# Decode forward and backward on one core: operands kept in SBUF, mat-vecs and weight gradients moved to TensorE

## The chip, the core and the metric

The kernel runs on one core of a Trainium2 chip. The metric is device microseconds (us) of that core. Each kernel is run several times and the median is quoted. A run counts as fast when it lies within 1.5% of the fastest run of the same kernel. A single run of a kernel has the state "unknown" and is used here only for readings of its trace. In the text PE is TensorE, PEld its weight load, DVE VectorE, ACT ScalarE, POOL GpSimd and SP SyncE. "The clock" is the share of TensorE's full clock that was granted, as the trace records it: 0.50 or 1.00 in nearly every stretch below.

## The reference

One token passes through attention, MLP, the same attention and the same MLP again (called A1, B2, A3, B4 below). Then the gradients of everything are taken. All tensors are bf16.

```python
def _A_ref(x, k_cache, v_cache, wq, wo):          # D 1024, 32 heads of 128, 4 KV heads, cache of 32768
    W = 4096                                      # only the last 4096 positions of the cache are used
    q = (x @ wq).reshape(B, Sq, Hq, Dh).transpose(0, 2, 1, 3)
    k = jnp.repeat(k_cache[:, :, Sk - W:, :], rep, axis=1)
    v = jnp.repeat(v_cache[:, :, Sk - W:, :], rep, axis=1)
    p = softmax(einsum("bhqd,bhkd->bhqk", q, k) * Dh ** -0.5)
    return einsum("bhqk,bhkd->bhqd", p, v).transpose(...).reshape(B, Sq, Hq * Dh) @ wo
def _B_ref(x, w1, b1, w2):                        # F 3584
    h = x @ w1 + b1
    return (h * tanh(softplus(h))) @ w2
x = x + _A_ref(layernorm(x), ...); x = x + _B_ref(layernorm(x), ...)     # and both once more
# outputs: x, and the gradients of x, k_cache, v_cache, wq, wo, w1, b1, w2 for a given grad_out
```

Three facts shape the work. Every product with a weight is a mat-vec. Every weight gradient is a sum of two outer products, one for each use of the weight, so it has rank two. And 58.7 MB of the gradients of the two caches, those of the positions that were not used, are zeros that must be written.

## The kernel before

In the forward part the mat-vecs were already done on PE, 128 columns of weight at a time. In the backward part they were products and sums along the free axis, on DVE and ACT, because there the contraction runs along the other axis of the weight. Each weight was loaded anew at every use, and K and V were loaded three times each, twice as they are and once transposed by the DMA.

```python
    # forward, for example q: a chunk of weight, 32 matmuls of one column each
    for t in range(TD):
        chunk = wpool.tile([P, J], BF16, name="wq_chunk")
        nc.sync.dma_start(chunk[:], wq_v[:, t, :])
        for h in range(HQ):
            nc.tensor.matmul(q_ps[:, c:c + 1], lhsT=chunk[:, h * P:(h + 1) * P], rhs=n_bf[:, t:t + 1], ...)
    # ... (cut)
    # backward: a mat-vec is a product with a broadcast row, summed by DVE, or by ACT after DVE
    def mv_accum(in0, in1, acc, n, prodpool):
        path = MV_PATTERN[mv_state[0] % len(MV_PATTERN)]          # "BABBA"
        if path == "A":
            nc.vector.tensor_tensor_reduce(out=prod[:, 0:n], in0=in0, in1=in1, ..., accum_out=acc)
        else:
            nc.vector.tensor_tensor(out=prod[:, 0:n], in0=in0, in1=in1, op=ALU.mult)
            nc.scalar.activation(prod[:, 0:n], prod[:, 0:n], ACT.Copy, accum_out=acc)
    # ... (cut)
    # a weight gradient: one pass of ACT, one of DVE, one output DMA
    def dw_block(ot, bc_hi, sc_hi, bc_lo, sc_lo, out_ap):
        nc.scalar.activation(ot, bc_hi, ACT.Copy, scale=sc_hi)
        nc.vector.scalar_tensor_tensor(out=ot, in0=bc_lo, scalar=sc_lo, in1=ot, op0=ALU.mult, op1=ALU.add)
        eng.dma_start(out_ap, ot)
```

Of the kernel before, what the change touches and what calls it, by code (L numbers as in the profile page):

```python
# [12 lines left out]
AX = mybir.AxisListType  # L13

# [3 lines left out]


def prow(h: int) -> int:  # L20
    return 32 * (h // 8) + (h % 8)
# [3 lines left out]
def kernel(  # L25
# [23 lines left out]

    D = A_x.shape[2]  # L50
    assert D % P == 0
    TD = D // P
    G = A_k_cache.shape[1]
    Sk = A_k_cache.shape[2]
    assert A_k_cache.shape[3] == DH
    assert G == 4, "kernel assumes 4 kv heads (one quadrant per group)"
    W = min(4096, max(256, Sk // 4))
    assert W % P == 0
    SC = min(512, W)
    assert W % SC == 0  # L60
    TK = W // P
    J = A_wq.shape[1]
    assert J == HQ * DH
    F = B_w1.shape[1]
    assert F % 512 == 0
    TF = F // P
    ZR = Sk - W
    assert ZR % P == 0
    scale = float(DH) ** -0.5
    eps = 1e-5  # L70
    invD = 1.0 / D

    keep = ctx.enter_context(tc.tile_pool(name="keep", bufs=1))
    ps1 = ctx.enter_context(tc.tile_pool(name="ps1", bufs=4, space=bass.MemoryType.PSUM))

    ident_bf = keep.tile([P, P], BF16, name="ident_bf")
# [3 lines left out]
    ones_f = keep.tile([P, P], FP32, name="ones_f")  # L80
    nc.vector.memset(ones_f[:], 1.0)
    ones_bf = keep.tile([P, P], BF16, name="ones_bf")
    nc.vector.memset(ones_bf[:], 1.0)
    eps_t = keep.tile([P, 1], FP32, name="eps_t")
    nc.vector.memset(eps_t[:], eps)


    KVT = keep.tile([P, G, W], BF16, name="KVT")

    zero_jobs = []  # L90
    if ZR > 0:
        per_part_z = ZR // P * DH
        for out_t in (out_2, out_3):
            for g in range(G):
                zero_jobs.append((out_t, g))

    def write_zero_regions(src_tile, njobs, name):
        if ZR == 0 or not zero_jobs or njobs == 0:
            return
        ZC = 1024 if per_part_z % 1024 == 0 else min(D, per_part_z)  # L100
        assert per_part_z % ZC == 0 and src_tile.shape[1] >= ZC
        zt = keep.tile([P, ZC], BF16, name=f"zt_{name}")
        nc.vector.tensor_scalar(out=zt[:], in0=src_tile[:, 0:ZC], scalar1=0.0, scalar2=None, op0=ALU.mult)
        reps = per_part_z // ZC
        for _ in range(njobs):
            if not zero_jobs:
                break
            out_t, g = zero_jobs.pop(0)
            dst = out_t[0, g, 0:ZR, :].rearrange("(p r) d -> p (r d)", p=P)
            nc.gpsimd.dma_start(dst.rearrange("p (r c) -> p r c", c=ZC), zt[:, None, :].to_broadcast([P, reps, ZC]))  # L110

    def load_col_f32(ap_flat, name):
        tb = keep.tile([P, TD], BF16, name=name + "_bf")
        nc.sync.dma_start(tb[:], ap_flat.rearrange("(t p) -> p t", p=P))
        tf = keep.tile([P, TD], FP32, name=name)
        nc.vector.tensor_copy(tf[:], tb[:])
        return tf

    x0 = load_col_f32(A_x[0, 0, :], "x0")
    gcol = load_col_f32(grad_out[0, 0, :], "gcol")  # L120

    b1_bf = keep.tile([P, TF], BF16, name="b1_bf")
    nc.sync.dma_start(b1_bf[:], B_b1.rearrange("(t p) -> p t", p=P))
    b1_f = keep.tile([P, TF], FP32, name="b1_f")
    nc.vector.tensor_copy(b1_f[:], b1_bf[:])

    db1_acc = keep.tile([P, TF], FP32, name="db1_acc")
    nc.vector.memset(db1_acc[:], 0.0)
# [4 lines left out]
    w2_v = B_w2.rearrange("(t p) d -> p t d", p=P)  # L133

    def ln_fwd(x_col, name):
        with tc.tile_pool(name=f"ln_{name}", bufs=1) as lp, tc.tile_pool(
            name=f"lnps_{name}", bufs=1, space=bass.MemoryType.PSUM
        ) as lps:
            xx = lp.tile([P, 2 * TD], FP32, name="xx")
            nc.vector.tensor_copy(xx[:, 0:TD], x_col[:])  # L140
            nc.vector.tensor_mul(xx[:, TD:2 * TD], x_col[:], x_col[:])
            sps = lps.tile([P, 2 * TD], FP32, name="sps")
            nc.tensor.matmul(sps[:], lhsT=ones_f[:], rhs=xx[:], start=True, stop=True)
            s12 = lp.tile([P, 2], FP32, name="s12")
            nc.vector.reduce_sum(s12[:], sps[:].rearrange("p (a b) -> p a b", a=2), axis=AX.X)
            mean = lp.tile([P, 1], FP32, name="mean")
            nc.vector.tensor_scalar(out=mean[:], in0=s12[:, 0:1], scalar1=invD, scalar2=None, op0=ALU.mult)
            msq = lp.tile([P, 1], FP32, name="msq")
            nc.vector.tensor_mul(msq[:], mean[:], mean[:])
            var = lp.tile([P, 1], FP32, name="var")  # L150
            nc.vector.scalar_tensor_tensor(out=var[:], in0=s12[:, 1:2], scalar=invD, in1=msq[:], op0=ALU.mult, op1=ALU.subtract)  # L151
            rstd = keep.tile([P, 1], FP32, name=f"rstd_{name}")
            nc.scalar.activation(rstd[:], var[:], ACT.Sqrt, bias=eps_t[:, 0:1], scale=1.0)  # L153
            nc.vector.reciprocal(rstd[:], rstd[:])
            n32 = keep.tile([P, TD], FP32, name=f"n32_{name}")
            nc.vector.tensor_scalar(out=n32[:], in0=x_col[:], scalar1=mean[:, 0:1], scalar2=rstd[:, 0:1], op0=ALU.subtract, op1=ALU.mult)
            n_bf = keep.tile([P, TD], BF16, name=f"nbf_{name}")
            nc.vector.tensor_copy(n_bf[:], n32[:])
        return n32, n_bf, rstd

    def ln_bwd(dn_col, n32, rstd, name):
        with tc.tile_pool(name=f"lnb_{name}", bufs=1) as lp, tc.tile_pool(
            name=f"lnbps_{name}", bufs=1, space=bass.MemoryType.PSUM
        ) as lps:
            tt = lp.tile([P, 2 * TD], FP32, name="tt")
            nc.vector.tensor_copy(tt[:, 0:TD], dn_col[:])
            nc.vector.tensor_mul(tt[:, TD:2 * TD], dn_col[:], n32[:])  # L167
            sps = lps.tile([P, 2 * TD], FP32, name="sps")
            nc.tensor.matmul(sps[:], lhsT=ones_f[:], rhs=tt[:], start=True, stop=True)  # L169
            ab = lp.tile([P, 2], FP32, name="ab")  # L170
            nc.vector.reduce_sum(ab[:], sps[:].rearrange("p (a b) -> p a b", a=2), axis=AX.X)
            nc.vector.tensor_scalar(out=ab[:], in0=ab[:], scalar1=invD, scalar2=None, op0=ALU.mult)
            nb = lp.tile([P, TD], FP32, name="nb")
            nc.vector.tensor_scalar(out=nb[:], in0=n32[:], scalar1=ab[:, 1:2], scalar2=None, op0=ALU.mult)
            t2 = lp.tile([P, TD], FP32, name="t2")
            nc.vector.tensor_sub(t2[:], dn_col[:], nb[:])
            gx = lp.tile([P, TD], FP32, name="gx")
            nc.vector.tensor_scalar(out=gx[:], in0=t2[:], scalar1=ab[:, 0:1], scalar2=rstd[:, 0:1], op0=ALU.subtract, op1=ALU.mult)
            gx_keep = keep.tile([P, TD], FP32, name=f"gx_{name}")
            nc.vector.tensor_copy(gx_keep[:], gx[:])  # L180
        return gx_keep

    def col_to_row(col_bf, ncols, dst_row_ap, rng, name):
        with tc.tile_pool(name=f"c2r_{name}", bufs=1, space=bass.MemoryType.PSUM) as rps:
            rowps = rps.tile([P, ncols * P], BF16, name="rowps")
            for c in range(ncols):
                nc.tensor.transpose(rowps[rng:rng + 1, c * P:(c + 1) * P], col_bf[:, c:c + 1], ident_bf[:], tile_position=(0, rng))
            nc.vector.tensor_copy(dst_row_ap[rng:rng + 1, :], rowps[rng:rng + 1, :])

    def col_to_row_mapped(colpad_bf, dst_row_ap, rng, name):  # L190
        with tc.tile_pool(name=f"c2rm_{name}", bufs=1, space=bass.MemoryType.PSUM) as rps:
            rowps = rps.tile([P, HQ * P], BF16, name="rowps")
            for h in range(HQ):
                c = prow(h)
                nc.tensor.transpose(rowps[rng:rng + 1, h * P:(h + 1) * P], colpad_bf[:, c:c + 1], ident_bf[:], tile_position=(0, rng))
            nc.vector.tensor_copy(dst_row_ap[rng:rng + 1, :], rowps[rng:rng + 1, :])

    def row_to_bcast(src_row_ap, rng, length, dst_bc, name):
        CB = min(512, length)
        assert length % CB == 0  # L200
        with tc.tile_pool(name=f"bc_{name}", bufs=2, space=bass.MemoryType.PSUM) as bps:
# [21 lines left out]
    def attn_fwd(x_col, lname, stack_row_n, stack_row_o, load_kt=False):  # L223
# [5 lines left out]
        with tc.tile_pool(name=f"qf_{lname}", bufs=1) as qp, tc.tile_pool(  # L229
# [16 lines left out]
            for g in range(G):  # L246
                nc.tensor.transpose(rows_ps[32 * g:32 * g + 32, :], qs_col[:, 32 * g:32 * g + 32], ident_bf[:], tile_position=(0, 32 * g))
# [433 lines left out]
```

## Time and profile before

| | before |
|---|---|
| time, median (lowest to highest) | 989.47 us (988.42 to 991.69), 3 runs |
| forward, backward, gradients | 0 to 323, 323 to 820, 820 to 991 us |
| bytes moved | 250.16 MB |
| busiest engine | DVE, 45% of the span |

First, lines of the profile's page. The rows of digits cut the span into 40 slices; a digit is the busy share of that slice in tenths (for PEclk, the clock in tenths). GB/s is what the DMA moved in each slice. The lines that start with L are groups of instructions: busy us, mean ns of one, then the idle time just before them and what ended it.

```profile
PE 270.3 (27%) x3388; PEld 197.5 (20%) x3388; DVE 446.1 (45%) x666; ACT 363.9 (37%) x568; POOL 17.7 (2%) x24
...
PEclk9956555567555555555655555555556755555555
...
GB/s 307 239 49 210 309 229 326 330 212 156 299 268 298 173 418 421 179 393 418 201 88 337 167 417 415 147 216 310 408 333 85 189 235 70 228 232 190 195 179 223
DMA packets 114187, 250.16 MB, mean 252 GB/s; under 512 B 48097, under 2 KB 48097, under 8 KB 105953
...
L459 ACT ACTIVATE mv_prod<-mv_prod 128x1024 bf16<-128x1024 bf16 (+2 forms) x91 | 137.8, 1515 | 182.5 <-DVE mv_prod L458 179.6
...
L563 DVE SCALAR_TENSOR_TENSOR dwo_ot<-gbcA_A_4276,ocol_A_740,dwo_ot 128x1024 bf16<-128x1024 bf16 x32 | 40.5, 1281 | 12.4 <-ACT dwo_ot L562 12.2
```

No engine is busy for half of the span, and the DMA reaches 415 GB/s and more in only five of 40 slices. The backward mat-vecs are the group at L459 with its DVE partner; the weight gradients are groups like L563, in which DVE waits for ACT.

Second, windows of the trace of before. Each row is a stretch of time: its bounds, its length, then busy us and number of instructions of PE, PEld, DVE, ACT and POOL, then the clock, the DMA share and GB/s.

```profile
66.00:78.00 12.00, 12.00 (x55) 5.98 (x55) 3.07 (x14) 3.69 (x14) 0.00 (x0) 0.50 0.01 1
...
234.00:240.00 6.00, 3.12 (x54) 2.94 (x54) 0.00 (x0) 0.00 (x0) 0.00 (x0) 1.00 0.62 238
360.00:396.00 36.00, 3.78 (x28) 2.89 (x28) 14.99 (x25) 18.22 (x25) 0.00 (x0) 0.50 1.03 420
820.00:991.00 171.00, 68.51 (x510) 54.01 (x508) 131.37 (x161) 126.45 (x239) 4.28 (x8) 0.50 0.55 191
```

Between 66 and 78 us TensorE does transposes in turn with small matmuls, each transpose with a copy before its result can be used, and the clock is 0.50. Between 360 and 396 us the DMA is full, at 420 GB/s, with zero writes beside loads. The gradients take 171 us with DVE and ACT busy for three quarters of it and the DMA about half used.

### The profile page before, as it was taken

What the parts mean: (1) busy time and instruction counts of PE and PEld (TensorE: products, weight loads), DVE (VectorE), ACT (ScalarE), POOL (GpSimd) and SP (SyncE); (2) the same over time, 40 slices, a digit from 0 to 9 for tenths busy, and PEclk for the clock granted to TensorE, in tenths of its full rate; (3) what the DMA queues carried; (4) which work ended last, traced back from release to release, by engine and by line L of the source; (5) the groups of instructions that cost most, each with busy time, mean ns of one, the idle gap of its engine ahead of it and who ended that gap; (6) DMA issues with size and microseconds to landing.
All of it is one profiled execution on the core that took longest, in us unless ns stands there. A gap on an engine that the chain in (4) does not pass through costs nothing. (4 is left out here: it accounts for less than half of the span.)

```text
span 991.2 us, 8850 instructions
## 1 busy us (share of the span) xinstructions
PE 270.3 (27%) x3388; PEld 197.5 (20%) x3388; DVE 446.1 (45%) x666; ACT 363.9 (37%) x568; POOL 17.7 (2%) x24
## 2 busy tenths in 40 slices
PE   2436323436322001000390001000005702234553
PEld 2224222314222001000160001000002501223432
DVE  1040101040010344764517545487644196897777
ACT  0030010020010236643116433336531256867776
POOL 0000000000000100010000100001000000000000
PEclk9956555567555555555655555555556755555555
DMA  8915868894878999599428499958982465554545
GB/s 307 239 49 210 309 229 326 330 212 156 299 268 298 173 418 421 179 393 418 201 88 337 167 417 415 147 216 310 408 333 85 189 235 70 228 232 190 195 179 223
DMA packets 114187, 250.16 MB, mean 252 GB/s; under 512 B 48097, under 2 KB 48097, under 8 KB 105953
## 3 DMA queue, kind: packets, MB, share of 16 engines
q1 hardware_dynamic: 93056, 166.76, 51.1%
q0 software_dynamic: 15616, 67.11, 16.6%
q10 hardware_dynamic: 5472, 15.73, 4.1%
q8 instruction: 26, 0.43, 0.2%
q14 instruction: 17, 0.13, 0.0%
HBM read 142.62 MB, written 98.58 MB: 243 GB/s over the span
## 5 line engine op out<-in xcount | busy, mean ns | idle before, releaser
L459 ACT ACTIVATE mv_prod<-mv_prod 128x1024 bf16<-128x1024 bf16 (+2 forms) x91 | 137.8, 1515 | 182.5 <-DVE mv_prod L458 179.6
L607 PE MATMUL kv_ps<-qsrows_A_1663,ds_A_3438 8*128 8x128 bf16 x128 | 29.8, 283 | 66.7 <-ACT kv_otile L612 33.6
L563 DVE SCALAR_TENSOR_TENSOR dwo_ot<-gbcA_A_4276,ocol_A_740,dwo_ot 128x1024 bf16<-128x1024 bf16 x32 | 40.5, 1281 | 12.4 <-ACT dwo_ot L562 12.2
L563 DVE SCALAR_TENSOR_TENSOR dwq_ot<-dqbc_A_4716,n_A_114,dwq_ot 128x4096 bf16<-128x4096 bf16 x8 | 35.8, 4480 | 9.7 <-ACT dwq_ot L562 9.7
L562 ACT ACTIVATE dwo_ot<-gbcA_A_3445,ocol_A_2278 128x1024 bf16<-128x1024 bf16 x32 | 36.2, 1152 | 10.6 <-DMA out_dram<-dwo_ot 10.6
L563 DVE SCALAR_TENSOR_TENSOR dwo_ot<-gbc_B_4017,a_B_1360,dwo_ot 128x1024 bf16<-128x1024 bf16 x28 | 35.6, 1282 | 9.7 <-ACT dwo_ot L562 9.5
L169 PE MATMUL sps<-tt,ones_f 128*128 128x16 f32 x8 | 2.3, 370 | 136.0 <-DVE tt L167 136.0
L563 DVE SCALAR_TENSOR_TENSOR dw_ot<-dhbc_B_4149,n_B_1072,dw_ot 128x3584 bf16<-128x3584 bf16 x8 | 31.6, 3949 | 16.6 <-ACT dw_ot L562 16.6
L612 ACT CAST kv_otile<-kv_ps 128x128 bf16<-128x128 f32 x170 | 35.2, 269 | 10.3 <-PE kv_ps L608 4.0
L219 PE MATMUL bfc_ps<-ident_bf,dh_bf 128*128 128x128 bf16 x56 | 7.5, 303 | 113.6 <-DVE dh_bf L429 61.8
L490 PE MATMUL dorows_ps<-ident_bf,do_col 128*32 128x128 bf16 x8 | 0.6, 288 | 133.8 <-DVE do_col L486 133.8
L607 PE MATMUL kv_ps<-dorows_A_3439,pbf_4866 8*128 8x128 bf16 x128 | 29.4, 286 | 28.0 <-DVE kv_otile L610 15.4
L153 ACT ACT_TABLE_LOAD x4 | 5.1, 1283 | 86.0 <-DVE var L151 85.3
L562 ACT ACTIVATE dw_ot<-dhbc_B_3317,n_B_2614 128x3584 bf16<-128x3584 bf16 x8 | 26.2, 3276 | 26.8 <-DMA out_dram<-dw_ot 26.7
L562 ACT ACTIVATE dwo_ot<-gbc_B_3185,a_B_2902 128x1024 bf16<-128x1024 bf16 x28 | 32.1, 1156 | 7.5 <-DMA out_dram<-dwo_ot 7.3
L523 PE MATMUL dq_ps<-kn,dsT_all 128*32 128x128 bf16 x256 | 33.3, 284 | 3.5 <-DMA kn<-in_A_k_cache_dram 3.2
L562 ACT ACTIVATE dwq_ot<-dqbc_A_3884,n_A_1656 128x4096 bf16<-128x4096 bf16 x8 | 29.7, 3714 | 11.8 <-DMA out_dram<-dwq_ot 11.1
L608 PEld LDWEIGHTS <-ds_A_4269 8*128 8x128 bf16 x128 | 19.1, 149 | 74.3 <-issue 73.5
L294 PE MATMUL o_ps<-vn,pT_all 128*32 128x128 bf16 x256 | 31.9, 271 | 4.6 <-DMA vn<-in_A_v_cache_dram 4.6
L608 PE MATMUL kv_ps<-qsrows_A_121,ds_A_4269 8*128 8x128 bf16 x128 | 32.4, 308 | 0.0
L608 PE MATMUL kv_ps<-dorows_A_4270,pbf_4868 8*128 8x128 bf16 x128 | 31.5, 307 | 0.0
L169 PEld LDWEIGHTS sps<-tt,ones_f 128*128 128x128 f32 x8 | 2.0, 311 | 136.8 <-issue 75.6
(266 smaller groups left out, 762.7 us busy)
## 6 DMA issues: line engine op xcount, KB each, us to landing
wq_chunk<-in_A_wq_dram SPq DMA_DIRECT2D x32, 1024.0 KB, 7.0
wo_chunk<-in_A_wo_dram SPq DMA_DIRECT2D x32, 1024.0 KB, 8.5
w_chunk<-in_B_w_dram SPq DMA_DIRECT2D x32, 896.0 KB, 6.7
w_chunk<-in_B_w_dram SPq DMA_DIRECT2D x28, 1024.0 KB, 8.8
out_dram<-zt_B_3202 POOLq DMA_DIRECT2D x2, 7168.0 KB, 56.4
out_dram<-zt_A_3462 POOLq DMA_DIRECT2D x2, 7168.0 KB, 42.3
out_dram<-zt_B_4034 POOLq DMA_DIRECT2D x2, 7168.0 KB, 44.9
out_dram<-zt_A_4293 POOLq DMA_DIRECT2D x2, 7168.0 KB, 46.1
```

The lines of the kernel that those rows point to most:

```text
L153: nc.scalar.activation(rstd[:], var[:], ACT.Sqrt, bias=eps_t[:, 0:1], scale=1.0)
L169: nc.tensor.matmul(sps[:], lhsT=ones_f[:], rhs=tt[:], start=True, stop=True)
L219: nc.tensor.matmul(bp[:, i * P:(i + 1) * P], lhsT=col_bf[:, src:src + 1].to_broadcast([P, P]), rhs=ident_bf[:], start=True, stop=True, til ...
L294: nc.tensor.matmul(o_ps[32 * g:32 * g + 32, :], lhsT=pT_all[:, t, 32 * g:32 * g + 32], rhs=vn[:, t, :], start=(t == 0), stop=(t == TK - 1) ...
L459: nc.scalar.activation(prod[:, 0:n], prod[:, 0:n], ACT.Copy, accum_out=acc)
L490: nc.tensor.transpose(rows_ps[32 * g:32 * g + 32, :], do_col[:, 32 * g:32 * g + 32], ident_bf[:], tile_position=(0, 32 * g))
L523: nc.tensor.matmul(dq_ps[32 * g:32 * g + 32, :], lhsT=dsT_all[:, t, 32 * g:32 * g + 32], rhs=kn[:, t, :], start=(t == 0), stop=(t == TK - ...
L562: nc.scalar.activation(ot, bc_hi, ACT.Copy, scale=sc_hi)
L563: nc.vector.scalar_tensor_tensor(out=ot, in0=bc_lo, scalar=sc_lo, in1=ot, op0=ALU.mult, op1=ALU.add)
L607: nc.tensor.matmul(ps[:], lhsT=X3[32 * g:32 * g + 8, t:W:TK], rhs=Y3[32 * g:32 * g + 8, :], start=True, stop=False, tile_position=(32 * g, 0))
L608: nc.tensor.matmul(ps[:], lhsT=X1[32 * g:32 * g + 8, t:W:TK], rhs=Y1[32 * g:32 * g + 8, :], start=False, stop=True, tile_position=(32 * g, 0))
L612: nc.scalar.copy(otile[:, t, :], ps[:])
```

## The change

The intent is to load wq, K and V once and keep them in SBUF, to transpose weights in place on PE where the other layout is wanted, so that the backward mat-vecs are PE work too, and to make each weight gradient by a matmul whose contraction is over two rows. DVE and ACT then only copy results out of PSUM. The diff rewrites nearly the whole kernel; its core is this.

```diff
+    def xpose_unit(ap2d, nb):                     # transposes 8 blocks, copies them back over themselves
+        ps = pt.tile([P, 8, P], BF16, name="tps", tag="pt")
+        for b in range(nb):
+            nc.tensor.transpose(ps[:, b, :], ap2d[:, b * P:(b + 1) * P], ident_bf[:])
+        evac(ap2d, ps[:, 0:nb, :].rearrange("p b c -> p (b c)"), 0.08 * nb, 0.12 * nb)    # DVE or ACT
     # ... (cut) attention forward
+        if first:
+            load_wq()
+            load_kv(K_t, k_v, "K")
     # ... (cut) at the end of each attention forward
+        for c in range(HQ // 2):
+            w = strm.tile([P, 2, D], BF16, name="wo_c", tag="st")
+            nc.sync.dma_start(w[:], wo_v[:, 2 * c:2 * c + 2, :])
+            if c == NB - 1:
+                zeros(10)                         # ten of 56 zero writes of 1 MB, in pieces of 1 KB
     # ... (cut) a backward mat-vec: load, transpose, one-column matmuls
-                        mv_accum(chunk[:, tt, :], gbc[:], da[:, t:t + 1], D, prodpool)
+            for tt in range(2):
+                xpose_unit(w[:, tt, :], 8)
+            for tt in range(2):
+                t = 2 * c + tt
+                for dch in range(TD):
+                    mm(dacc[:, t:t + 1], w[:, tt, dch * P:(dch + 1) * P], g_bf[:, dch:dch + 1], dch == 0, dch == TD - 1)
     # ... (cut) gradients: the two vectors of each weight lie in two rows of ROWS
+    ROWS = keep.tile([P, 5120], BF16, name="ROWS")
-        nc.scalar.activation(ot, bc_hi, ACT.Copy, scale=sc_hi)
-        nc.vector.scalar_tensor_tensor(out=ot, in0=bc_lo, scalar=sc_lo, in1=ot, op0=ALU.mult, op1=ALU.add)
+                mm(ps[:], ROWS[base:base + 2, (r0 + rr) * P:(r0 + rr + 1) * P], ROWS[base:base + 2, L + i * 512:L + (i + 1) * 512],
+                   True, True, tile_position=(base, 0))
+                ev_out(st[:, rr, i * 512:(i + 1) * 512], ps[:])
     # ... (cut) order of the end
+    zeros(100)                                    # all that are left
+    to_row(sB4["a_bf"], TF, 96, 0, "a4")          # column -> row, by a small DMA into ROWS
     # ... (cut)
+    for t in range(0, TF, 2):
+        dw_tall(96, t, 4096, out_8.rearrange("(t p) d -> p t d", p=P), "w2")
     # ... (cut) then w1, wo, V, K and wq, each with its own to_row calls just ahead
```

## The prediction

> **What bounds the kernel now.** No single engine: the summary page shows DVE busy 45% of 991 us, ACT 37%, PE 27%. The stage windows show three regimes.
> - Forward, 0 to 323 us: mat-vec stages run at the DMA ceiling. A chunk of 32 column mat-vecs takes 1.02 us (31.5 ns each, at granted clock 0.5 and 1.0 alike) and then PE waits for the next chunk. Windows full of loads move 380 to 422 GB/s. Each attention adds about 50 us with little DMA (4096-column softmax, 64 transposes handed over one by one).
> - Backward, 323 to 820 us: mat-vecs are products on DVE and ACT (1.22 us, or 0.69 + 1.24 us, per 128x1024 block; 128x4096 costs 4.42 us). Zero writes beside loads fill windows at 415 to 420 GB/s and starve DVE; wq and w1 stages are DVE-bound; the attention middle (744 to 792 us) has little DMA.
> - Gradients, 820 to 991 us: each block needs an ACT pass (1.15 us per 128x1024) and a DVE pass (1.28 us), alternating with output DMA in the chain of waits. DMA is half used.
>
> **What the change does.**
> - Traffic falls from 250 MB (DMA view) to about 204 MB: wq, K, V once (17 MB), streamed wo, w1, w2 89 MB, zeros 59 MB, outputs 40 MB. At the 418 GB/s seen here: 488 us, the floor.
> - Backward mat-vecs go to TensorE: 1920 more at 31.5 ns = 60 us, but each block first needs a transpose: about 2050 in all. Eight back-to-back 128-column matmuls (the broadcasts) took 1.04 us at clock 0.5, so about 107 ns each at half clock: 220 us; 120 us if the clock is granted. Evacuating 128x1024 bf16 from PSUM, extrapolated from 225 ns (DVE) and 266 ns (ACT) for 128 columns, is 0.69 and 1.0 us; shared, 0.41 us per 8 transposes, below PE.
> - Attention middles shrink: 1024-column softmax rows, a fourth of the exp and reduction time.
> - Gradients: 312 evacuations of 512 columns (0.69 us DVE, 0.59 us ACT): 99 us shared. PE 160 us at half clock, 80 us at full.
>
> The Trainium skill, "TensorE: Matmul & The Clock Gate", Part 4, says that transposes do not bring the full clock. This trace agrees weakly: interleaved transposes (66 to 78 us) stayed at 0.50 with PE busy throughout, while plain dense matmuls (234 to 240 us) reached 1.0. I assume half clock in the backward streams.
>
> **Sum of estimates (us):** A1 forward 90 (36 MB with ten zero writes, DMA-bound), B2 36, A3 48, B4 36: 210. Backward MLPs 30 chunks x 2.3 = 69 + 6 each; A3 backward 37 (wo) + 58 (resident transposes) + 33; A1 backward 70: about 350, PE-bound, zeros hidden below. Gradients 100 to 150, partly overlapped. Total about 670; with full clock about 560. I take 640.
>
> **What would show it.** Forward windows at 400 GB/s or more with PE waiting for DMA; backward windows with PE near full, clock 0.5, DMA under half, transposes near 107 ns apart; gradients with DVE and ACT near full; total DMA near 204 MB; PE the largest share in the chain of waits.
>
> **What would make it wrong.** Full clock during transposes (then 560); transposes waiting for evacuation with only four PSUM buffers, or mat-vecs waiting in order behind copies (700 or more); rank-2 matmuls at half clock setting the last phase; 512 KB loads falling short of 400 GB/s.
>
> Predicted 640 us, 80% range 560 to 735. Faster by over 2%: 0.98; within 2%: 0.01; slower: 0.01.

## The result, and the profile after

| | before | after |
|---|---|---|
| time, median (lowest to highest) | 989.11 us (988.42 to 991.69), 4 runs | 653.39 us (652.58 to 653.72), 4 runs |
| forward | 323 us | 225 us |
| backward | 497 us | 230 us |
| gradients | 171 us | 197 us |
| bytes moved | 250.16 MB | 205.10 MB |

The ratio is 0.6595, with a 95% interval of 0.6579 to 0.661. The ratios here and below are those of fast runs over fast runs; they are not quite the ratios of the medians in the tables. The time of before differs a little from the first table because a fourth run was added with the result. The results are correct.

The total was predicted within 14 us. The stages were not: the backward part was predicted at about 350 us, and the gradients at 100 to 150. The last stage even became 26 us longer than the one it replaced.

The same lines of the page, for after:

```profile
PE 451.2 (69%) x7117; PEld 325.0 (50%) x7117; DVE 242.1 (37%) x470; ACT 203.4 (31%) x292; POOL 62.3 (10%) x109
...
PEclk9985555555555599989975999995555555555555
...
GB/s 307 425 415 383 388 286 390 388 386 383 388 387 392 252 281 333 296 283 382 382 390 153 289 288 298 304 384 382 384 390 195 289 185 309 218 195 139 153 224 292
DMA packets 118215, 205.10 MB, mean 315 GB/s; under 512 B 11514, under 2 KB 68992, under 8 KB 117120
...
L145 PE MATMUL ops<-ROWS 2*128 2x512 bf16 (+1 forms) x248 | 104.8, 606 | 29.8 <-DMA ROWS<-rt 26.3
...
L138 PE MATMUL tps<-ident_bf,w_c 128*128 128x128 bf16 x896 | 72.1, 225 | 0.0
L133 ACT COPY w_c<-tps 128x896 bf16<-128x896 bf16 (+1 forms) x48 | 45.8, 955 | 79.7 <-PE tps L138 74.6
L130 DVE COPY w_c<-tps 128x1024 bf16<-128x1024 bf16 (+1 forms) x72 | 47.0, 656 | 46.1 <-PE tps L138 35.2
```

PE is now the busiest engine. The row PEclk has the main surprise in it: digits of 7 to 9, with one 5 between, from the 15th to the 27th slice, and nothing but 5 after that. A slice is 16.3 us, so these are the backward stages (228 to 440 us). The clock was full where the prediction took half, and half where PE had the most to do. The group at L145 is the weight gradients: PE stood still before them for 29.8 us, and 26.3 us of that ended with a small copy into ROWS.

The windows of after, with the columns as above:

```profile
12.00:24.00 12.00, 4.97 (x140) 4.23 (x136) 0.00 (x0) 0.00 (x0) 0.00 (x0) 1.00 1.03 420
60.00:84.00 24.00, 0.00 (x0) 0.00 (x0) 0.00 (x0) 0.00 (x0) 0.00 (x0) 0.50 1.08 389
240.00:324.00 84.00, 76.60 (x1538) 69.65 (x1535) 50.13 (x85) 47.94 (x51) 0.00 (x0) 0.98 0.98 338
312.00:324.00 12.00, 12.00 (x219) 12.00 (x217) 10.69 (x18) 10.16 (x12) 0.00 (x0) 1.00 1.09 383
336.00:348.00 12.00, 9.45 (x336) 9.14 (x334) 0.69 (x1) 0.20 (x1) 0.00 (x0) 0.50 0.99 366
360.00:432.00 72.00, 60.73 (x1272) 51.58 (x1269) 34.24 (x61) 33.03 (x34) 0.00 (x0) 1.00 0.92 306
504.00:516.00 12.00, 12.00 (x33) 4.48 (x32) 9.26 (x16) 8.82 (x17) 3.82 (x7) 0.50 0.61 240
588.00:612.00 24.00, 24.00 (x127) 16.32 (x124) 10.20 (x17) 9.80 (x17) 5.25 (x8) 0.50 0.46 167
```

Read them in order. In the forward part the DMA is full and PE waits for it; between 60 and 84 us PE does nothing at all, because the next chunk's load stands behind ten zero writes. From 240 to 324 and from 360 to 432 us PE is busy for five sixths and more, at full clock. From 312 to 324 us it does only the transposes of resident operands: 219 instructions in 12 us are 55 ns each. From 336 to 348 us it does almost only matmuls of one column (for wq) or eight (for K), and the clock is back at 0.50. In the gradients, 504 to 516 and 588 to 612 us, PE is busy without a gap, and the clock is 0.50 all the same.

The timeline of PE in the trace of after, at the start of the backward part (start, us, engine and operation, number):

```profile
225.83 2.85 PE L138 MATMUL tps<-ident_bf,w_c 128*128 128x128 bf16 x25
228.47 0.40 PE L145 MATMUL acc<-gcolb,w_c 128*128 128x1 bf16 x8
...
230.14 0.77 PE L138 MATMUL tps<-ident_bf,w_c 128*128 128x128 bf16 x11
...
231.14 0.38 PE L138 MATMUL tps<-ident_bf,w_c 128*128 128x128 bf16 x4
```

One transpose alone takes 0.27 us at half clock and 0.22 us at full clock, from its start to its end; the next one starts sooner than that. The first 25 take 2.85 us, so they start about 107 ns apart. Later eleven take 0.77 us and four 0.38 us, so they start about 55 ns apart. In windows of 1 us the clock is 0.50 up to 229 us, 0.67 in the next and 1.00 from 230 us, about 4 us after the first transpose; the work until then was transposes with a few one-column mat-vecs between them. From 302 to 330 us PE does nothing but transposes, and the clock stays at 1.00 (the window 312 to 324 us above), so transposes alone keep it there.

The end of the chain of waits of after, in order of time (start, us, what):

```profile
615.97 2.36 DMA ROWS<-rt
...
618.58 27.37 PE ops L145 x64
```

The last weight's 64 matmuls take 27.37 us, so they follow each other every 0.43 us, behind a copy of its rows. Nothing else is in the chain there: it is PE alone that sets the pace.

### The profile page after: what moved, and what is told of

The parts are those of the page before. It is cut to its first block, busy times and chain, and to the rows that moved or that the text cites. A ratio compares the mean times of both kernels' runs of the same rounds, so it can differ in the third digit from the quotient of the medians.

```text
span 652.0 us, 16240 instructions
## 1 busy us (share of the span) xinstructions
PE 451.2 (69%) x7117; PEld 325.0 (50%) x7117; DVE 242.1 (37%) x470; ACT 203.4 (31%) x292; POOL 62.3 (10%) x109
## 2 busy tenths in 40 slices
DMA packets 118215, 205.10 MB, mean 315 GB/s; under 512 B 11514, under 2 KB 68992, under 8 KB 117120
## 5 line engine op out<-in xcount | busy, mean ns | idle before, releaser
L145 PE MATMUL ops<-ROWS 2*128 2x512 bf16 (+1 forms) x248 | 104.8, 606 | 29.8 <-DMA ROWS<-rt 26.3
L145 PEld LDWEIGHTS <-w_c 128*128 128x128 bf16 x1792 | 60.2, 101 | 67.3 <-DMA w_c<-in_B_w_dram 40.5
L145 PEld LDWEIGHTS <-ROWS 2*128 2x128 bf16 x248 | 33.6, 137 | 99.7 <-issue 88.9
L138 PE MATMUL tps<-ident_bf,w_c 128*128 128x128 bf16 x896 | 72.1, 225 | 0.0
L133 ACT COPY w_c<-tps 128x896 bf16<-128x896 bf16 (+1 forms) x48 | 45.8, 955 | 79.7 <-PE tps L138 74.6
L145 PEld LDWEIGHTS <-wo_c 128*128 128x128 bf16 x1024 | 33.3, 101 | 63.8 <-DMA wo_c<-in_A_wo_dram 45.0
L130 DVE COPY w_c<-tps 128x1024 bf16<-128x1024 bf16 (+1 forms) x72 | 47.0, 656 | 46.1 <-PE tps L138 35.2
L138 PEld LDWEIGHTS <-w_c 128*128 128x128 bf16 x896 | 54.1, 100 | 0.1
L130 DVE CAST st_t<-ops 128x512 bf16<-128x512 f32 x57 | 39.0, 691 | 28.3 <-PE ops L145 21.5
L130 DVE CAST st_w<-ops 128x448 bf16<-128x448 f32 (+1 forms) x60 | 39.5, 658 | 21.1 <-PE ops L145 19.0
L133 ACT CAST st_w<-ops 128x448 bf16<-128x448 f32 (+1 forms) x68 | 37.1, 560 | 29.0 <-PE ops L145 27.1
L138 PE MATMUL tps<-ident_bf,wo_c 128*128 128x128 bf16 x512 | 39.9, 223 | 0.0
L133 ACT COPY wo_c<-tps 128x1024 bf16<-128x1024 bf16 x26 | 26.3, 1012 | 33.6 <-PE tps L138 29.8
L145 PE MATMUL acc<-obf_A_787,wo_c 128*128 128x1 bf16 x256 | 8.5, 166 | 32.8 <-DMA wo_c<-in_A_wo_dram 30.9
L138 PEld LDWEIGHTS <-wo_c 128*128 128x128 bf16 x512 | 30.4, 99 | 0.0
L145 PE MATMUL ops<-do3x,p_A_1983 32*128 32x256 bf16 x64 | 23.7, 414 | 0.8 <-DVE do3x L213 0.8
## 6 DMA issues: line engine op xcount, KB each, us to landing
out_dram<-zt SPq DMA_DIRECT2D x56, 1024.0 KB, 10.8
```

What stands on the lines that cost most here:

```text
L130: nc.vector.tensor_copy(out_ap, in_ap)
L133: nc.scalar.copy(out_ap, in_ap)
L138: nc.tensor.transpose(ps[:, b, :], ap2d[:, b * P:(b + 1) * P], ident_bf[:])
L145: nc.tensor.matmul(out_ap, lhsT=lhsT, rhs=rhs, start=start, stop=stop, skip_group_check=True, **kw)
```

## The experiments

Two questions were open. Why are the gradients at half clock with PE full, and what would they cost without that? And where did the time go that the prediction's DMA floor (488 us, an estimate from 204 MB at 418 GB/s) left over? Twelve kernels were run. The first four were each meant to change one thing.

### e1_zeros_late: the forward part without zero writes

```diff
             if c == NB - 1:
-                zeros(10)
+                zeros(0)
```

> The 20 zero writes of 1 MB that stand in the two forward attentions are issued with the last ones instead (40 at the end). Theory A, the forward pass is bound by DMA traffic and the gradient phase by TensorE at half clock with DMA half idle: PE's idle stretch of 24.4 us in the first attention and the like in the second go away, the forward pass falls from 225 us to about 180, the gradient phase grows by less than 15 us (longer waits for the small row copies), total 608 to 625. Rival, total DMA traffic is what binds everywhere: total unchanged within 1% (647 to 660).

Measured: 652.76 us (649.85 to 653.97), ratio 0.6583 (0.656 to 0.6605). Nothing was gained, as the rival had it, though the backward streams began some 30 us sooner. Windows of this run:

```profile
60.00:84.00 24.00, 8.94 (x228) 7.70 (x228) 1.48 (x10) 0.50 (x2) 0.00 (x0) 0.50 0.94 316
...
456.00:540.00 84.00, 45.58 (x116) 15.03 (x115) 32.33 (x59) 29.01 (x56) 21.29 (x36) 0.50 1.06 399
```

PE works between 60 and 84 us now. But the twenty writes went to the end of the list, and there the DMA is full from about 396 to 540 us. Between 456 and 540 us PE is busy for 45.58 us; in the kernel after it was 58.83 us in the same window, at a DMA share of 0.77. The stall was moved, not removed. That by itself does not show that the stall was free, nor that the total traffic binds everywhere, as the rival says; e10_zeros_late_data returns to it.

### e2_row_groups: gradient matmuls in turn over four groups of rows

The vectors of the four weights lie in rows 0, 32, 64 and 96, so their matmuls use different rows of the PE array. In the kernel after they are issued one weight after the other. Here they are issued in turn, and so are the four quarters of the K and V gradients. To do so the results are also collected in more tiles on their way out.

```diff
+    def dw_all():
+        for u in range(16):
+            units = [dw_unit(k, u) for k in ("w2", "wo", "w1", "wq") if not (k == "w2" and u >= TF // 2)]
+            for i in range(4):
+                for step, _ in units:
+                    step(i)                       # one matmul and its copy out of PSUM
+            for _, out in units:
+                out()
     # ... (cut) dkv: the loop over c, the row group, is now the innermost; all to_row calls come first
```

> The gradient matmuls (2 rows, and 32 rows for K and V) are issued in turn over the four 32-row groups of the array instead of group after group; same work, same results. Theory P, the last phase (192 us) is bound by PE streaming 512 columns in 0.43 us at half clock one after another: they overlap up to four deep, the phase becomes bound by evacuation (312 at 0.32 us, 99 us) plus the first wait for row copies, 120 to 135 us, total 580 to 600; clock stays 0.5. Rival E, evacuation, PSUM buffers or output DMA bind: total 640 to 660. Rival R, row groups do not overlap: unchanged as well, with matmuls still 0.43 us apart.

Measured: 628.27 us (627.37 to 628.59), ratio 0.6338 (0.6323 to 0.6354): 25 us gained where 53 to 73 were expected. Windows of this run, and a line of its PE timeline:

```profile
457.00:482.00 25.00, 4.86 (x20) 1.81 (x20) 5.27 (x23) 0.58 (x1) 8.67 (x17) 0.50 0.98 342
504.00:576.00 72.00, 54.47 (x175) 12.73 (x173) 52.35 (x83) 50.23 (x94) 27.84 (x44) 0.50 0.80 302
```

```profile
482.26 0.61 PE L145 MATMUL ops<-ROWS 2*128 2x512 bf16 x4 [1.51 <-DMA ROWS<-rt]
```

Most of the waiting for row copies is still there, gathered at the head: from 457 to 482 us PE is busy for 4.86 of 25 us. After that, 175 matmuls in 72 us are 0.41 us each. In the kernel after, 64 of 512 columns took 27.65 us and 64 of 448 columns 24.50 us, which is 0.42 us in this mix of three to one. So little was gained, but PE is no longer full: it waits for copies out of PSUM (11.6 us for ACT's copies of the weight gradients, 6.4 us for DVE's). The groups do overlap: at 482.26 us four matmuls in four groups start within 0.03 us and end after 0.61 us, where four in one group, 0.58 us for one and 0.43 us for each more, would take about 1.87 us (an estimate from the kernel after). After such a four the matmuls wait for their four PSUM buffers to be emptied; e7_groups_banks tests how much that costs. The K and V part took about 49 us.

### e5_behind: mat-vecs one chunk behind the transposes

In the backward streams a chunk's mat-vecs need its transposes copied back, and PE works in order. Here the mat-vecs of a chunk are issued after the transposes of the next.

```diff
             for tt in range(2):
                 xpose_unit(w[:, tt, :], 8)
-            for tt in range(2):
-                ...
+            def mv(w=w, c=c):
+                ...                               # the same matmuls
+            behind(mv)                            # runs the closure of the chunk before, holds this one
+        behind(None)
```

> In the backward streams the mat-vecs of a chunk are issued one chunk later, behind the next chunk's transposes. Theory L, PE waits in order for the copies of its own transposes (about 0.5 us per 0.5 MB chunk, PE idle 2 us of 12): a w1 chunk goes from 1.7 to about 1.3 us, total 615 to 635. Rival D, the DMA engines (share 0.86 to 0.96 in these windows at 300 GB/s) are the bound of the streams: total unchanged, 648 to 656, and PE waits for loads instead.

Measured: 637.37 us (636.92 to 637.89), ratio 0.6432: 16 us gained, 2 us outside of the range expected. The same window of after, then of this run:

```profile
240.00:300.00 60.00, 52.63 (x1099) 45.88 (x1096) 30.11 (x53) 27.97 (x29) 0.00 (x0) 0.97 0.93 320
```

```profile
240.00:300.00 60.00, 55.82 (x1224) 53.45 (x1221) 34.56 (x62) 33.33 (x36) 0.00 (x0) 0.97 0.99 353
```

PE runs 1224 instructions in place of 1099, a gain of 11%, and then the DMA is full (0.99). Waiting in order behind copies was real; the gain ends where the loads cannot come faster.

### e6_rows_early: rows written as soon as their columns exist

```diff
     g3, g3b = mlp_bwd(gcol, gcol_bf, "B4", sB4)
+    to_row(sB4["a_bf"], TF, 96, 0, "a4")          # eleven of the sixteen, moved up from the gradients
+    ...
     g2, g2b = attn_bwd(g3, g3b, "A3", sA3, True)
+    to_row(g2b, TD, 97, 4096, "g2")               # and so on, each after its column
```

> The 16 small copies that lay columns out as rows are issued in the backward pass, as soon as their columns exist, not at the head of each gradient. Theory: PE's 26 us of waits for them in the gradient phase are all on the path: total 630 to 640. Rival: the waits only shift to PSUM and staging buffers: total above 645.

Measured: 641.59 us (640.12 to 643.0), ratio 0.647: 12 us gained, again just outside of the range. In its trace PE no longer waits for a row copy at all in the gradients; the largest sum of waits there is 6.8 us for copies out of PSUM, in four waits. The 26.3 us of waits were worth 12 us and not 26. The likely reason is that the gradients now begin while the last zero writes still fill the DMA (share 1.05 at 405 GB/s between 480 and 504 us, PE busy for 17.87 of 24 us).

### e3_rows128 and e4_rows64: what brings the clock up

Their outputs are wrong, which doesn't matter for the times. The gradient matmuls contract over all 128 rows, or over 64, in place of 2 (weights) and 32 (K and V). ROWS is zero at first, so in the first weight's part 126 of the 128 rows are zeros.

```diff
-                mm(ps[:], ROWS[base:base + 2, ...], ROWS[base:base + 2, ...], True, True, tile_position=(base, 0))
+                mm(ps[:], ROWS[0:0 + 128, ...], ROWS[0:0 + 128, ...], True, True, tile_position=(0, 0))
     # e4_rows64: rows (base // 64) * 64 to + 64, at that tile position; the K and V gradients likewise
```

> Wrong results on purpose. The gradient matmuls run over all 128 rows of the array: at first 126 of them are zeros for the w2 gradient, and for K and V all hold data. Same number of columns streamed, same evacuations. Theory H, the clock follows how many rows of the array are in use: it rises to 1.0 within a few us of the phase, matmuls of 512 columns come 0.22 us apart when they do not wait, phase 192 us to about 130-150 us (evacuation 99 us and the waits for row copies, which get longer because the rows now share one region). Rival Z, what counts is data that is not zero: 0.5 in the w2 part, 1.0 for K and V. Rival S, the phase is slow for another reason than rows (short bursts, waits): 0.5 throughout, total near 653.

> Wrong results on purpose. As the run with 128 rows, with 64. Theory H: between 32 rows (0.5 in the kernel as it is, with PE busy all the time) and 128; if the activity is measured in proportion to rows with a threshold near half, it is the borderline; I expect 0.5 to 0.75 and no more than a small gain. Rivals Z and S as there.

Measured: 631.13 us and 657.7 us, one run each (state unknown). In the run over 128 rows, a window of the first weight's part, a window of the K and V gradients and the timeline of PE in it; then a window of the run over 64 rows:

```profile
488.00:496.00 8.00, 5.74 (x24) 2.00 (x22) 6.91 (x14) 5.37 (x10) 3.98 (x6) 0.98 0.93 340
...
576.00:588.00 12.00, 11.31 (x103) 9.85 (x101) 8.10 (x12) 7.64 (x15) 4.29 (x6) 1.00 0.92 243
```

```profile
576.07 0.27 PE L145 MATMUL ops<-q3x,ds_A 128*128 128x256 bf16 x1
576.18 0.27 PE L145 MATMUL ops<-q1x,ds_A 128*128 128x256 bf16 x1
```

```profile
588.00:612.00 24.00, 23.16 (x114) 15.51 (x114) 10.76 (x22) 8.19 (x14) 5.00 (x7) 0.50 0.41 146
```

Over 128 rows the clock reaches 1.00 in every part, some 3 to 6 us after PE starts to work there, and falls back to 0.50 where PE waits for row copies or stands still for 2 to 3 us. At full clock the matmuls of 256 columns follow every 0.11 us; in the kernel after, over 32 rows, they follow every 0.21 us. In the first weight's part, with 126 rows of zeros, the matmuls begin at 469 us; the clock is 0.50 up to 474 us, 1.00 at 476 to 478 us, half again after a wait, and 1.00 from 486 to 494 us. So zero data do not hold it down; in these kernels it goes with the rows that a matmul addresses. Over 64 rows nothing changed: clock 0.50, and 64 matmuls of 512 columns in 27.66 us, as over 2 rows. The rival, that zero data leave the array idle as far as the clock is concerned, has fallen. Nothing between 64 and 128 rows was tried, and no run tells the number of rows apart from the fact that a matmul over 128 rows takes the array undivided. The time is a miss: 22 us less, where a phase of 130 to 150 us in place of 192 meant 42 to 62. At full clock PE waits again, in this run's gradients 30.6 us for row copies and 16.4 us for ACT's copies out of PSUM.

### e7_groups_banks: the row groups with all eight PSUM banks

```diff
+    bank, wide = [0], [None]
     def dw_psum(n=512):
-        return pt.tile([P, 512], FP32, name="ops", tag="pt")
+        i = bank[0] % 8
+        ...                                       # four from pt in turn with four that are free by then
```

> As the run with row groups in turn (628.3 us), with eight PSUM banks for the gradients instead of four. Theory B: there, four matmuls fill four banks together and the next four wait for two engines to empty them; in the K and V part 64 blocks took 49 us, 0.77 us each, where two engines could do 0.32. With eight banks filling and emptying overlap: K and V part 49 to about 28 us, the weight part 95 to about 85, total 590 to 608. Rival D, output DMA or the staging tiles bind: total above 620.

Measured: 615.16 us (614.21 to 617.18), ratio 0.6182 (0.6148 to 0.6215): 13 us less than e2_row_groups, and 5 us short of the range. The waits for PSUM were part of it. From 504 to 528 us 65 matmuls take 24 us, 0.37 us each, at clock 0.50, and now PE is busy for 22.64 of 24 us.

### e8_zeros_in_dkv: an experiment that did not do what was meant

The ten zero writes of A1 were to go between the outputs of the K and V gradients, where the DMA is half used, from POOL's queue.

```diff
-                zeros(10)
+                zeros(0 if first else 10)
     # ... in dkv, after each output
+                if zero_jobs:
+                    nc.gpsimd.dma_start(zero_jobs.pop(0), zt[:, None, :].to_broadcast([P, 8, ZC]))
```

> The kernel as it is, but the ten zero writes of the first attention are issued between the outputs of the V and K gradients, where the DMA share is 0.4 and PE is busy all the time. Theory: moving zero writes early to late brought nothing (652.8 us) because they landed where DMA was full already (396 to 550 us at 380 to 405 GB/s, PE waiting); moved to where DMA has room they are worth the 24 us that PE stood idle in the first attention: total 625 to 635. Rival: the start of the kernel is bound by something else and the time is unchanged (650 to 655).

Measured: 655.76 us (654.58 to 657.37). It says nothing about the question. The writes depend on nothing but the zero tile, so the build moved them ahead on POOL's queue to the very start of the kernel, as the first window of its trace shows:

```profile
0.00:12.00 12.00, 2.37 (x50) 2.02 (x50) 2.33 (x14) 1.78 (x3) 8.42 (x17) 1.00 0.74 244
```

Of the 17 things that POOL does in these 12 us eight are zero writes, and the last two follow by 20 us; the loads of wq then share the DMA with them. The same bytes in the forward part cost the same time.

### e10_zeros_late_data: the same, with a dependency

```diff
+    zt2 = work.tile([P, ZC], BF16, name="zt2", tag="e32", padded_shape=[P, 2 * WC])
+    nc.vector.tensor_scalar(out=zt2[:], in0=do3[:].rearrange("p g d -> p (g d)"), scalar1=0.0, scalar2=None, op0=ALU.mult)
     # ... in dkv, after each output
+                if zero_jobs:
+                    nc.gpsimd.dma_start(zero_jobs.pop(0), late[0][:, None, :].to_broadcast([P, 8, ZC]))
```

> The retry of the run whose zero writes were hoisted to the start: the same ten writes of 1 MB are taken out of the first attention and issued between the outputs of the K and V gradients, this time from a zero tile that is computed from a late column, so that they cannot start early. Theory M (a transfer costs its time where the DMA is full and nothing where it is half idle): the first attention loses the 24.4 us for which the PE stood still, the K/V gradients have DMA to spare (share 0.37 to 0.5), total 626 to 636 us. Rival (the writes are paid wherever they stand, because the gradients' own outputs queue behind them, or because what follows the stall is bound elsewhere): 645 us or more.

Measured: 634.91 us (633.84 to 639.57), ratio 0.64 (0.6381 to 0.6419): 18.5 us less than the kernel after. Windows of this run:

```profile
60.00:72.00 12.00, 4.70 (x128) 4.04 (x128) 0.00 (x0) 0.00 (x0) 0.00 (x0) 0.50 1.01 318
...
552.00:576.00 24.00, 23.16 (x122) 15.42 (x121) 11.21 (x22) 9.13 (x16) 11.38 (x15) 0.50 1.02 375
```

The stall of PE is gone, and the ten writes are issued between 542 and 577 us. PE goes on beside them, at 23.16 of 24 us in the second window and 18.54 of 24 us in the next 24 us; so about 6 of the 24.4 us came back. Together with e1_zeros_late this settles the point: a zero write costs its full time in a stretch that the DMA bounds, and little in one that PE bounds. The change had put twenty of 56 into the first kind, and e1_zeros_late moved them to another stretch of the same kind.

### e9_all: the parts that gained, together

The closures of e5_behind, the groups and banks of e7_groups_banks, the early rows of e6_rows_early, no zero writes in A1 (ten are spread over the backward MLP streams), and the K and V gradients ahead of the weights'. It is correct.

> All together: mat-vecs one chunk behind, row copies early, row groups in turn with eight banks, no zero writes in the first attention (ten spread over the streams of the two backward MLPs), K and V gradients ahead of the weight gradients so that the last zero writes run below them. If the gains of the parts add (16 + 12 + about 50 + 20 us off 653) about 555; DMA alone needs 205 MB at 385 GB/s, 532 us, and cannot be full all the time, so I expect 550 to 580. Rival: the parts all gain the same waits for DMA and the total stays above 590.

Measured: 588.37 us (585.66 to 592.21), ratio 0.591 (0.5872 to 0.5948), 8 us outside of the range. The single gains over the kernel after, 38 for groups and banks, 16 and 12, with the stall's 18.5, would add up to about 85 us; 65 came. A likely reason is in the trace: its DMA is full, 1.02 to 1.09, from 420 to about 504 us, so that what was saved before may be waited for there. No run tests it.

### e11_all_128rows and e12_all_128rows_bigzeros: the clock, done correctly, and larger pieces

The run of 588 us with the weight gradients over all 128 rows, and this time correct. The stationary side lies in the three V tiles that are dead by then, set to zero but for each weight's own two rows, so the other rows of ROWS contribute nothing. In the second run the zeros are also written in pieces of 2 KB, as in the kernel before, in place of 1 KB.

```diff
+    LH = [V_t[i][:].rearrange("p t d -> p (t d)") for i in range(3)]
+    for i in range(3):
+        nc.vector.memset(LH[i][:, 0:(4096, 4096, 2048)[i]], 0.0)
+    to_row(sB4["a_bf"], TF, 96, 0, "a4", LH[0])   # and seven more; the moving side stays in ROWS
-            mm(ps[:, 0:n], ROWS[base:base + 2, lhs[i]:lhs[i] + P], ROWS[base:base + 2, rhs[i]:rhs[i] + n],
-               True, True, tile_position=(base, 0))
+            mm(ps[:, 0:n], LH[{96: 0, 32: 1}.get(base, 2)][:, lhs[i]:lhs[i] + P], ROWS[:, rhs[i]:rhs[i] + n], True, True)
 # e12_all_128rows_bigzeros, besides (and ROWS loses its unused first 1024 columns, for room)
-    ZC = 512
+    ZC = 1024
```

> The combination of 588 us, with one thing changed and correct results: the weight gradients are multiplied over all 128 rows, the stationary halves lying in the dead V tiles, zero outside their two rows. If the granted clock is what still holds the weight gradients (29 matmuls per 12 us at 0.50, DMA share 0.73 to 0.81 from 516 us on), the clock there is 1.00, the matmuls come at the rate of the copies out of PSUM (36 to 38 per 12 us) and the total is 562 to 576 us. Rival: the copies out of PSUM and the DMA already hold that stretch, and the row groups already overlap what the clock would give: 584 us or more.

> The run over 128 rows, with the zeros written in pieces of 2 KB instead of 1 KB. If the smaller pieces are why the DMA moves only 380 to 392 GB/s with the zeros in it, against 415 to 420 in the kernel before and 419 to 426 for loads alone here, the DMA-full stretches with zeros show over 405 GB/s and the total is 6 to 12 us under the run over 128 rows. Rival (the rate is set by writes mixed with loads, not by the piece): the same rate and the same time within 3 us.

Measured: 580.71 us (579.02 to 582.77), ratio 0.5858 (0.5837 to 0.5879), and 576.58 us (575.4 to 577.48), ratio 0.5814 (0.58 to 0.5829). The same window of the weight gradients in e9_all, then in e11_all_128rows:

```profile
528.00:540.00 12.00, 10.82 (x29) 2.21 (x28) 9.18 (x15) 6.96 (x15) 3.35 (x6) 0.50 0.84 318
```

```profile
528.00:540.00 12.00, 9.65 (x33) 3.06 (x32) 8.60 (x15) 8.85 (x18) 5.07 (x8) 1.00 0.82 307
```

The clock is full, as expected; the rate rose from 29 to 33 matmuls in 12 us, and not to the 36 or more that the copies out of PSUM would allow. The time fell by 7.7 us where 12 or more were expected. The two were timed on different chips, and their intervals touch, so the 7.7 us is the least certain of these differences; the clock and the rate in the traces are not in doubt. In this stretch no engine and not the DMA (0.82) is full any more. PE's recorded waits, 5.9 us between 516 and 564 us, are all for copies out of PSUM, but what holds the rate at 33 was not found out.

A stretch that the last zero writes fill, in e11_all_128rows, then in e12_all_128rows_bigzeros:

```profile
432.00:444.00 12.00, 8.75 (x144) 5.50 (x144) 4.96 (x21) 2.54 (x5) 1.60 (x4) 0.50 1.09 382
```

```profile
432.00:444.00 12.00, 8.76 (x135) 5.42 (x133) 4.96 (x21) 2.54 (x5) 1.99 (x4) 0.50 1.05 404
```

Twice the piece gives 404 GB/s for 382, and 4.1 us in total; 6 to 12 us were expected. The rate came out about as expected (over 405 was named); the time was overrated, presumably because part of the zero writes is not on the path any more. Another way that was not followed up: the ten zero writes that e8_zeros_in_dkv issues from POOL, in pieces of 1 KB as before, went out in about 2,700 packets, as its page counts them, where the queue of SP took 10,400, and the DMA moved 413 to 417 GB/s with them and loads from 12 to 48 us. 576.58 us is the fastest version found. At the 205.10 MB that it moves and the 404 GB/s that it reaches, an estimate of the DMA's own time is 508 us.

## Why the prediction was right, and where it was not

The total, 640 us predicted and 653.39 measured, was right because wrong terms cancelled. In the prediction's sum of 670 the gradients stand for about 110, once 210 and 350 are taken off. The backward part came out 120 us shorter, the gradients 87 us longer and the forward part 15 us longer. For the chance of full clock the prediction then took 30 us off its sum, and the three errors together make 18.

- **Forward, 210 us predicted, 225 measured.** The mechanism held: loads bound it and PE waits. The term that was off is the bandwidth. "Forward windows at 400 GB/s or more" held from 6 to 42 us (419 to 426 GB/s); with zero writes in pieces of 1 KB, and in the streams after them, it was mostly 383 to 398. Larger pieces brought the zero writes to 404. For the loads of wo, w1 and w2 in pieces of 512 KB no run shows the reason.
- **"I assume half clock in the backward streams": this step failed.** The trace shows 0.98 and 1.00 there, transposes 55 ns apart and not 107, and 230 us in place of 350. The Trainium skill, "TensorE: Matmul & The Clock Gate", Part 4, says that the full clock does not engage for transposes; here it did, about 4 us after the first. The trace of before had looked like agreement (66 to 78 us, clock 0.50), with PE recorded as busy throughout; but 55 instructions in 12 us, about half of them transposes and half small matmuls that need their results, are not dense. The lesson lies in the count beside the busy time: 219 instructions in 12 us after, 55 before. The branch "with full clock about 560" was named and given too little weight, and its sum would have been too low for the next point.
- **"Gradients 100 to 150, partly overlapped": this term was mis-sized.** The copies were costed right: 691 ns on DVE and 587 on ACT were measured, 0.69 and 0.59 us predicted. "PE 160 us at half clock" was in the text too, with "rank-2 matmuls at half clock setting the last phase" among what would make it wrong, and is about what PE took: 248 matmuls at 0.42 us and 256 at 0.213 us are 104 and 55 us. But the term was then set by the 99 us of copies. What the trace shows is that PE's time adds up, full at half clock with DVE and ACT waiting for it, and 26.3 us of waits for row copies that the prediction did not have at all. The experiments show each: 128 rows brought the clock to 1.00 (e3_rows128), early rows took the waits away (e6_rows_early), groups of rows with eight banks gave 38 us (e7_groups_banks). The full clock by itself was worth 22 us in e3_rows128 (one kernel, wrong), and 7.7 us on top of the other parts (e11_all_128rows).
- **"Zeros hidden below": half right.** For the sixteen in the backward part no run tests it. Those of A1 were costed in the forward part, where PE stood still for 24.4 us, as if that could not be helped. e10_zeros_late_data shows that 18.5 us of it could.
- **"Mat-vecs waiting in order behind copies" was named as a risk** of 700 us or more. It was real, and worth 16 us (e5_behind).
- **Traffic, 204 MB predicted, 205.10 measured:** right. "PE the largest share in the chain of waits": right, but the page follows that chain over little more than the last weight, 4% of the span. "DMA under half in the backward part": wrong with the clock, it was 0.92 to 0.98.

The skill's Part 1 of the same page ties the clock to how busy the PE has been. That describes the idle stretches here, but not the gradients: PE busy for 12.00 of 12 us over 2 rows, 0.50. And Part 3 gives 3.07 times for four row groups of 32 rows and 512 columns. Four free buffers at a time show about that factor here, 0.61 us for four matmuls against an estimated 1.87 (e2_row_groups). As a rate it does not last: with eight banks it came from 0.42 to 0.37 us a matmul, with PE busy for 22.64 of 24 us; whether only copies out of PSUM stand in the way was not tested further.

What stays open: what holds the weight gradients at 33 matmuls in 12 us once the clock is full, and why the clock stays at 1.00 for the first 42 us of the kernel, with one-column mat-vecs that keep PE busy less than half of the time (12 to 24 us), when denser matmuls of one and eight columns later run at 0.50 (336 to 348 us).

## What to carry to other kernels

Ask for each stretch of TensorE work not only how full it is but how many rows of the array it addresses, and look at the granted clock beside the busy time; a rank-two product padded with zeros to 128 rows can be faster than the same product over two (here by 7.7 us, in the runs that were correct). Put writes that nobody waits for into stretches that compute bounds, and make them depend on late data if they must stay there. Check a prediction stage by stage: a right total may be the sum of several wrong stages.

## What the Trainium skill lacked or had wrong

- "TensorE: Matmul & The Clock Gate", Part 4, says that the full clock does not engage for transposes. Here dense 128x128 bf16 transposes, which the trace records as MATMUL, brought it from 0.50 to 1.00 in about 4 us and kept it: about 107 ns apart at first, 55 ns later (219 transposes in 12 us). Whether these instructions run in the transpose mode that the page means, the trace does not show.
- The same page, Part 1, makes the clock a matter of how busy the PE is. Here matmuls of 256 to 512 columns over 2, 32 or 64 rows stayed at 0.50 with PE busy 12.00 of 12 us, and over 128 rows, 126 of them zeros, reached 1.00. Matmuls of one and eight columns over 128 rows with PE busy for 9.45 of 12 us ran at 0.50, so rows alone do not decide it either. No page gives the number of rows as a condition.
- "DMA: Bandwidth & Descriptors", "Why small descriptors are slow", reckons about three cycles for each packet beside one cycle for each 32 bytes. By that, an estimate for pieces of 1 KB and 2 KB is 35/32 and 67/64, a difference of 4.5%; the runs show 382 and 404 GB/s, 5.8%. The page works the loss out only for pieces of 256 bytes; here it can still be measured at 1 KB.
- The same page's section on bandwidth says that the HBM side, about 358 GB/s for one core, binds for transfers between HBM and SBUF, and gives 425 measured for 16 MB. Here, with one core at work, loads ran at 419 to 426 GB/s from 6 to 42 us, so 358 did not bind.
- No page has what a chain of transpose, copy and small DMA, several of them in a row, costs the engine that waits for it. One such DMA took 2.6 to 3.4 us here from issue to landing (medians by size), but the four waits of PE for them took 26.3 us, the longest 10.8 us.
